# Pairs of half-height matmuls moved between rounds of an attention and feed-forward kernel, with another last projection unit and two more warm-up passes

## The chip, the core and the metric

The kernel runs on one core of a Trainium2 chip. Its time is the device time of one execution in microseconds; each number for a kernel is the median of several executions. Five engines work side by side and are tied by semaphores: TensorE (PE, with its weight loads listed apart as PEld), VectorE (DVE), ScalarE (ACT), GpSimd (POOL) and SyncE (SP). PE accumulates in PSUM, of which there are eight banks of 128 x 512 float32; SP and POOL issue most DMAs.

## The reference

The input x has 2048 rows of 448 numbers. The result mixes an attention block and a gated feed-forward block by a gate for each row:

```python
g = sigmoid((x * gate_w).sum(-1, keepdims=True))
# a: 16 heads of 28, softmax(q k^T * 28**-0.5) v, then @ wo
# b: gate = x @ W_gate; up = x @ W_up; (relu(gate) * up) @ W_down, F = 1792
return g * a + (1 - g) * b
```

## The kernel before

**Precision.** Operands of projections are split into a high part (rounded to the matmul's format, by a copy on ACT, or on DVE) and a low part (the difference, by DVE or POOL). A product of 448 rows is then a chain of eleven matmuls, the list TERMS, each of 128 rows and 512 columns. Chunk 6 of the weights holds the last 64 rows twice, high in one half of the partitions and low in the other. The last term, (6, 7), needs only 64 rows. Two such last terms ("tails") of two units can stand in different halves of the array: SECOND is the set of units whose tail lies in the second half and whose partner is the unit before. Such a pair starts nearly at once; other tails use all 128 rows.

**Projection.** After a memset on DVE, WARM matmuls on zeros run while the first data arrive and are split. Then come units qk(tb, c) (eleven matmuls of 512 columns into one bank, a copy on ACT, a low part on DVE, a send to DRAM by POOL) and vproj(tb, t) (eleven of 450 columns, a copy of V and one of the gate column, both on ACT; behind each fourth unit two sends of V by POOL). The list `mixed` sets their order: 19 qk and 16 vproj units, from the third on in turn. Between the matmuls of the later ones stand the first maxima of scores (smax: two matmuls into a double bank from ps_w, then a maximum over 1024 on DVE) and the first 16 scores (EARLY: one matmul into a bank from ps_s, then an exponential on ACT).

**Attention rounds.** ROUNDS lists strings, and each letter is one step in PE's order: s is a score matmul with its exponential, m a smax, x one pass of a gate/up unit (unit number 2i is gate of block i, 2i+1 is up), u the second half of the first weights' split, h the tails that were left out of the passes. A gate unit ends with a relu into RL, an up unit with spill_h: a product with RL on DVE, into a buffer h, and a send to DRAM by POOL. LONG and WIDE have maxima; LATE, the last three rounds, has none. There scores come in pairs (scores_pair: two matmuls into a double bank of ps_w, one exponential over 1024 columns), and relu runs on DVE. Behind the letters of a round split_f makes the weights for the next round, and pv multiplies the exponentials of eight tiles with V, in groups of four matmuls of 32 output columns each, and adds the sum po to os (DVE, or a copy by ACT for a head's first half).

**PSUM.** Three rings of two: ps_s and ps_x of one bank each, ps_w of two banks each. A new tile of a ring waits for the readers of the last but one.

**Behind the attention.** gate_up(i) computes gate and up of a block into one ps_w tile (blocks 51 to 55); down(i) multiplies a loaded and split hidden block (hh) with W_down into four accumulators acc (L703); wout multiplies the attention's result with wo, and result mixes.

Of the kernel before, what the change touches and what calls it, by code (L numbers as in the profile page):

```python
# [26 lines left out]
NF = F // P  # L27
NB = 4
# [2 lines left out]
SCALE = DH ** -0.5  # L31
VC = D + 2
NQ = 2 * D // P
WARM = 9

EARLY = (5, 5, 4, 4, 4, 3, 3, 3, 2, 2, 2, 2, 1, 1, 1, 1)

# [2 lines left out]

FIRST = "s" * 12 + "mmssmxxsxxusxmxsxsmxsmxsxsmxsxsmxsxsmxsxsxmsxsxmsxsxmsx"

LONG = "mxsmsxxxxxsmsxsmsxxsmsxsmsxxsmxxsmsxsxxsmsxxsxsmxsxsmsxxsmsxsmsxxsmsxsxxsmsmxssh"
WIDE = "sxxmxmxxsxxmsxxsxsmxxssxmxmxsxxsxxsxsmsxxsmxssxxxsmsxxsxmsxmsxsxmsxsmxsxsxxsmsxxsmsmsxxsxsh"

LATE = "ssxxxssxxxssxxxssxx" * 2 + "ssxxxssxxxssxxssxx" * 2 + "h"

ROUNDS = [(FIRST, 2)] + ([(LONG, 3)] * 2 + [(WIDE, 4)]) * 2 + [(LONG, 3)] * 2  # L50

ROUNDS += ([(WIDE, 4)] + [(LONG, 3)] * 8) * 2 + [(LONG, 3)] * 2 + [(LATE, 4)] * 3
NP = 9
# [4 lines left out]
NT = len(TERMS)  # L58
# [9 lines left out]
def gated_mix_kernel(ctx, tc, x, wq, wo, wgu, wd, out):  # L68
# [8 lines left out]
    def f32(ap):  # L77
        return ap.bitcast(F32)
# [4 lines left out]
    def ps_w(name):  # L83
        return psum.tile([P, 2, TB], F32, tag="mx", bufs=2, name=name)

    def ps_x(name):
        return psum.tile([P, TB], F32, tag="x", bufs=2, name=name)
# [7 lines left out]
    def low(dst, src, high):  # L95
        nc.vector.tensor_tensor(dst, src, f32(high), op=OP.subtract)  # L96
# [98 lines left out]
    def xf(tb, b):  # L195
        return X[tb][b // 4][:, b % 4]
# [13 lines left out]
    with tc.tile_pool(name="qkv", bufs=1) as pa:  # L210
# [127 lines left out]
        ps = ps_x("warm_ps")  # L338
        for n in range(WARM):
            nc.tensor.matmul(ps, warm[:, :P], warm, start=True, stop=True)  # L340
# [38 lines left out]
        units = [(qk, 3, 1), (qk, 2, 2), (qk, 3, 2)]  # L379
        units += [(qk, tb, c) for c in range(3, NQ) for tb in range(NB - 1, -1, -1)]  # L380
        vs = [(vproj, tb, t) for tb in range(NB - 1, -1, -1) for t in range(4)]
        mixed = units[:2]
        units = units[2:]
        while units or vs:
            mixed += units[:1] + vs[:1]
            units, vs = units[1:], vs[1:]
        spills = {15 + 3 * k: (NB - 1 - k // 2, k % 2) for k in range(6)}
        m, first, ahead = 0, 9, 2 * LEAD + 4
        for n, (f, *a) in enumerate(mixed):
# [15 lines left out]
            among, ends = [], m  # L405
# [21 lines left out]
    att = stk.enter_context(tc.tile_pool(name="att", bufs=1))  # L427

    done = sum(n for _, n in ROUNDS) // 2
    SECOND = {sum(n for _, n in ROUNDS[:r + 1]) - 1 for r in range(len(ROUNDS)) if "h" in ROUNDS[r][0]}  # L430
    SECOND |= set(range(2 * done + 1, 2 * NB * NF, 2))

    def lane(k):
        return slice(64 * k, 64 * k + 64)

    def split_f(i, high, low, part=(0, 1)):

        if part[0] == 0:
            WS[i] = fe.tile([P, 2, 7, P], F32R, name=f"wg_{i}", tag="wg", bufs=2)
        w, wr = WS[i], WR[i]  # L440
        for s in part:
            high(w[:, s, 0:3], wr[:, s, 0:3])
            low(w[:, s, 3:6], wr[:, s, 0:3], w[:, s, 0:3])
        if part[-1] == 1:
            high(w[:, :, 6], wr[:, :, 3])
            for s in range(2):
                rows = lane(1 - (2 * i + s in SECOND))
                low(w[rows, s, 6], wr[rows, s, 3], w[rows, s, 6])
            del WR[i]
# [4 lines left out]
    def gu_mm(ps, i, s, n):  # L454

        a, b = (BY_CHUNK if i else HIGH_FIRST)[n]
        rows = slice(0, P)
        if n == NT - 1 and 2 * i + s in SECOND | {k - 1 for k in SECOND}:
            rows = lane(int(2 * i + s in SECOND))
        nc.tensor.matmul(ps, WS[i][rows, s, a], xf(i // NF, b)[rows], start=(n == 0), stop=(n == NT - 1))  # L460
        c = b % 4
        if i % NF == NF - 1 and s and i < NB * NF - 1 and (n == NT - 1 or BY_CHUNK[n + 1][1] % 4 != c):
            for r in range(2):
                nc.sync.dma_start(f32(X[0][r])[:, c], x_d[i // NF + 1, r][:, c])
# [20 lines left out]
    NI = H * NK  # L485
    OS, LS = {}, {}

    def pv(i0, ni, late):

        h = i0 // NK  # L490
        po = ps_x(f"po_{i0}") if late else ps_w(f"po_{i0}")[:, 0]
        for i in range(i0, i0 + ni):
            p = PT.pop(i)
            for j in range(NB):
                nc.tensor.matmul(po[32 * j:32 * j + 32], V[:, h // 4 % 2, i % NK, h % 4], p[:, j], start=(i == i0),  # L495
                                 stop=(i == i0 + ni - 1))
        if i0 % NK == 0:
            OS[h] = fe.tile([P, TB], F32, name=f"os_{h}", tag="os", bufs=2)
            nc.scalar.activation(OS[h], po, AF.Copy)
        else:  # L500
            nc.vector.tensor_tensor(OS[h], po, OS[h], op=OP.add)  # L501
        if (i0 + ni) % NK == 0:
            LS[h] = fe.tile([P, 16], F32, name=f"ls_{h}", tag="ls", bufs=2)
            nc.gpsimd.dma_start(LS[h], OS[h][DH::32].rearrange("j (p c) -> j p c", c=16))
# [26 lines left out]
    def load_wo():  # L531
        r = f32(q_slot("wor"))
        nc.sync.dma_start(r[:, 0:3, :D], wo_d[0:3 * P].rearrange("(c p) n -> p c n", p=P))
        for a in (0, 64):
            nc.sync.dma_start(r[a:a + 64, 3, :D], wo_d[3 * P:])
        return r[:, :, :D]
# [7 lines left out]
    nxt = parts = i0 = 0  # L544

    def small_things(u):

        h, q = divmod(u, 4)

        if q == 0 and h and h + 2 < H:  # L550
            load_k(h + 2)
            load_q(h + 2)
        if u in (16, 32):
            g = u // 16 + 1
            nc.sync.dma_start(V[:, g % 2], v_d[g])
        if u == 1:
            gates()
        if u == 2:
            pack_wo()
        if h and q == 1:  # L560
            row_sums(h - 1)
            spread(h - 1)
        if h and q == 2:
            normalise(h - 1)
# [4 lines left out]
    for r, (order, nu) in enumerate(ROUNDS):  # L569
        ni = order.count("s") // NB  # L570
        late = order == LATE
        todo = list(range(nxt, nxt + nu))
        nxt += nu
        small_things(i0 // 4)
        if m % (2 * NK) == 0 and i0 <= NI - LEAD:
            smax_end(m // (2 * NK) - 1)
        if late and wor is None:
            wor = load_wo()

        passes = [(*divmod(k, 2), n) for k in todo for n in range(NT - ("h" in order and k >= nxt - 2))]  # L580
        units = []
        ns = 0
        for o in order:
            if o == "x" and not passes:
                continue
            if o == "s":
                i, j = i0 + 1 + ns // NB, ns % NB
                if ns == 4 * NB:
                    small_things(i0 // 4 + 1)
                if len(EARLY) <= i * NB + j < NI * NB and not late:  # L590
                    scores(i, j)
                elif late and i < NI and j % 2 == 0:
                    scores_pair(i, j)
                ns += 1
            elif o == "m":
                smax(m)
                m += 1
            elif o == "x":
                i, half, n = passes.pop(0)
                if n == 0:  # L600
                    ps = (ps_s if late else ps_x)(f"gu_{i}_{half}")
                    units.append((i, half, ps))
                gu_mm(units[-1][2], i, half, n)
                if n == NT - 1:
                    i, half, ps = units.pop()
                    spill_h(i, ps) if half else relu(i, ps, late)
            elif o == "u":
                split_f(0, act_high, pool_low, (1,))
                load_k(2)
                load_q(2)  # L610
                fetch_f(2)
                parts = 2
            elif o == "h":
                for i, half, ps in units:
                    gu_mm(ps, i, half, NT - 1)
                for i, half, ps in units:
                    spill_h(i, ps) if half else relu(i, ps, late)
        assert not passes, (r, passes)

        ready = nxt + (ROUNDS[r + 1][1] if r + 1 < len(ROUNDS) else 2)  # L620
        ready += ready % 2
        while parts < ready:
            split_f(parts // 2, dve_high if late else act_high, pool_low, (parts % 2,))
            parts += 1
            if parts % 2 == 0:
                fetch_f(parts // 2 + 1)
        pv(i0, ni, late)
        i0 += ni
        if late and i0 == NI:
            split_wo(wor)  # L630
# [35 lines left out]
    def gate_up(i):  # L666
        if i + 1 < NB * NF:
            split_f(i + 1, act_high, low)
        if i + 3 < NB * NF:
            fetch_f(i + 3)  # L670
        ps = ps_w(f"gu_{i}")
        for s in range(2):
            for n in range(NT - 1):
                gu_mm(ps[:, s], i, s, n)
        for s in range(2):
            gu_mm(ps[:, s], i, s, NT - 1)
        relu(i, ps[:, 0])
        spill_h(i, ps[:, 1])

# [51 lines left out]
    todo = [(gate_up, done), (row_sums, H - 1), (gate_up, done + 1)]  # L731
# [12 lines left out]
    for tb, load, split, at in ((0, 2, (3, 4), (5, 6, 7, 8)), (1, 5, (7, 9), (10, 11, 14, 14)), (2, 21, (23, 25), (28,) * 4),  # L744
                                (3, 35, (37, 39), (42,) * 4)):
        before(load, (fetch_o, tb))
        for k, i in enumerate(split):
            n = todo.index((down, i))
# [53 lines left out]
```

## Time and profile before

| | |
|---|---|
| median of 3 runs | 1299.31 us (1298.84 to 1300.36) |
| the profiled execution's own time | 1299.74 us |
| its span, first to last instruction | 1297.6 us |
| PE / DVE / ACT / POOL busy | 1290.2 / 817.3 / 763.0 / 367.3 us |
| matmuls | 6685 |
| lines of the chain with the largest shares | gu L460 22%, sm L152 19%, po L495 17%, s L178 17%, acc L703 11% |
| mean DMA rate | 115 GB/s |

Busy times are unions of the instructions of an engine in one profiled execution. Ends of matmuls are modelled, so their starts are the firmer reading. A row of the timeline gives the start, the length of a merged group, the engine, the line, the operation and its tiles; in brackets stands how long the engine was idle before it and what ended that. A row of the waits gives the total in us, how many times, and the longest.

In the trace the first pass on zeros starts at 1.20 us, the first projection matmul at 5.71, the attention's first round at 143.74, and its first pv at 161.22. The three LATE rounds run from 1018.3 to 1092.3; gate_up(51) starts at 1092.26.

### The profile page before, as it was taken

How to read it: one execution, taken by the hardware profiler on the slowest of the kernel's cores; microseconds unless marked ns; L12 is line 12 of the kernel's file. 1: busy time of each engine (PE TensorE's matmuls, PEld its weight loads, DVE VectorE, ACT ScalarE, POOL GpSimd, SP SyncE). 2: the span in 40 equal slices, each digit the busy share in tenths (PEclk: the TensorE clock that was granted, in tenths of full speed). 3: DMA queues.
4: the chain of work that ended last, by engine and by line, in shares of the span. 5: the costliest groups of instructions: out<-in, count | busy, mean ns of one | idle time of the engine just before them, and what ended most of it. 6: DMA issues, size and time to landing. Idle time of an engine off the chain costs nothing.

```text
span 1297.6 us, 17707 instructions
## 1 busy us (share of the span) xinstructions
PE 1290.2 (99%) x6685; PEld 901.8 (69%) x6685; DVE 817.3 (63%) x849; ACT 763.0 (59%) x1387; POOL 367.3 (28%) x551
## 2 busy tenths in 40 slices
PE   9999999999999999999999999999999999999998
PEld 6888766666666666666666666666666656899997
DVE  6487766667677676777666667767677333663342
ACT  5212776666767777777776666767676755322121
POOL 3222122332313222222223322313132354641020
PEclk9999999999999999999999999999999999999999
DMA  9845523151427223141535142422341222744432
GB/s 311 293 159 230 154 75 98 57 122 47 118 66 192 73 78 99 54 100 47 135 104 121 57 104 69 110 68 82 78 135 35 92 82 88 247 136 151 135 109 77
DMA packets 53565, 148.87 MB, mean 115 GB/s; under 512 B 10024, under 2 KB 17128, under 8 KB 48872
## 3 DMA queue, kind: packets, MB, share of 16 engines
q1 hardware_dynamic: 36120, 98.34, 28.3%
q0 software_dynamic: 16928, 48.93, 10.4%
q8 instruction: 53, 0.87, 0.3%
q10 hardware_dynamic: 432, 0.46, 0.1%
q14 instruction: 32, 0.26, 0.1%
HBM read 102.06 MB, written 46.02 MB: 114 GB/s over the span
## 4 chain that ended last, share of the span: by engine, by line
PE 99%; DMA 0%; ACT 0%; DVE 0%; issue 0%; ACTq 0%
PE gu L460 22%; PE sm L152 19%; PE po L495 17%; PE s L178 17%; PE acc L703 11%; PE qk L303 6%; PE v L313 3%; PE wo L657 3%; PE s L189 2%; DMA wr<-wq 0%; PE mt L162 0%; DVE mx L154 0%; DVE pair L96 0%; DVE y L709 0%; ACT pair L90 0%
## 5 line engine op out<-in xcount | busy, mean ns | idle before, releaser
L154 DVE TENSOR_REDUCE mx<-sm 128x1 f32<-128x1024 f32 x512 | 614.2, 1221 | 107.5 <-PE sm L152 107.3
L180 ACT ACTIVATE P<-s 128x512 f32<-128x512 f32 x724 | 414.8, 598 | 164.0 <-PE s L178 124.0
L460 PE MATMUL gu<-X,wg 128*128 128x512 f32 (+1 forms) x1232 | 392.3, 402 | 0.0
L178 PE MATMUL s<-Q,K 114*128 114x512 f32 x932 | 368.7, 401 | 0.0
L152 PE MATMUL sm<-K,Q 112*128 112x512 f32 x1024 | 324.0, 398 | 1.6 <-DVE mx L154 1.6
L460 PEld LDWEIGHTS gu<-X,wg 128*128 128x128 f32 (+1 forms) x1232 | 226.4, 189 | 55.3 <-issue 10.7
L178 PEld LDWEIGHTS s<-Q,K 114*128 114x128 f32 x932 | 175.2, 188 | 89.0 <-ACT P L180 47.7
L152 PEld LDWEIGHTS sm<-K,Q 112*128 112x128 f32 x1024 | 192.2, 190 | 46.9 <-issue 10.1
L495 PE MATMUL po<-P,V 128*32 128x512 f32 x1600 | 181.0, 594 | 0.0
L482 POOL DMA_DIRECT2D h_d<-h x56 | 31.6, 563 | 524.9 <-DVE h L476 441.0
L99 POOL TENSOR_TENSOR wg<-wgr,wg 128x384 fp32r<-128x384 f32 x204 | 146.8, 737 | 8.1
L180 ACT ACTIVATE V<-s 128x512 f32<-128x512 f32 x208 | 119.6, 598 | 42.0 <-PE s L178 30.4
L703 PE MATMUL acc<-WD,hh 128*128 128x448 f32 x672 | 141.1, 368 | 0.0
L703 PEld LDWEIGHTS acc<-WD,hh 128*128 128x128 f32 x672 | 125.8, 188 | 13.3 <-ACT wg L90 0.5
L495 PEld LDWEIGHTS po<-P,V 128*32 128x32 f32 x1600 | 49.5, 110 | 111.2 <-issue 110.5
L90 ACT ACTIVATE hh<-hr 128x512 fp32r<-128x512 f32 x56 | 35.4, 632 | 124.8 <-PE acc L703 119.4
L96 DVE TENSOR_TENSOR hh<-hr,hh 128x512 fp32r<-128x512 f32 x56 | 46.6, 832 | 65.7 <-ACT hh L90 65.7
L303 PE MATMUL qk<-X,W 128*128 128x512 f32 x308 | 79.7, 402 | 0.6 <-ACT X L90 0.5
L303 PEld LDWEIGHTS qk<-X,W 128*128 128x128 f32 x308 | 59.0, 193 | 15.6 <-ACT X L90 1.4
L501 DVE TENSOR_TENSOR os<-po,os 128x512 f32<-128x512 f32 x16 | 11.1, 691 | 86.2 <-PE po L495 81.3
L96 DVE TENSOR_TENSOR mh<-mr,mh 16x128 fp32r<-16x128 f32 x16 | 6.0, 375 | 90.8 <-ACT mh L166 90.8
L90 ACT ACTIVATE wg<-wgr 128x384 fp32r<-128x384 f32 x150 | 60.3, 491 | 2.4 <-DMA wgr<-wgu 2.4
(74 smaller groups left out, 767.1 us busy)
## 6 DMA issues: line engine op xcount, KB each, us to landing
wgr<-wgu SPq DMA_DIRECT2D x55, 512.0 KB
K<-qk_d SPq DMA_DIRECT2D x64, 224.0 KB
Q<-qk_d SPq DMA_DIRECT2D x64, 224.0 KB
h_d<-h POOLq DMA_DIRECT2D x56, 256.0 KB, 2.3
hr<-h_d SPq DMA_DIRECT2D x56, 256.0 KB
qk_d<-st POOLq DMA_DIRECT2D x21, 512.0 KB, 3.6
x_d<-X POOLq DMA_DIRECT2D x6, 1024.0 KB, 5.2
X<-x_d SPq DMA_DIRECT2D x24, 256.0 KB
```

Of the source, the lines that this page charges most:

```text
L90: nc.scalar.activation(dst, src, AF.Copy)
L96: nc.vector.tensor_tensor(dst, src, f32(high), op=OP.subtract)
L99: nc.gpsimd.tensor_tensor(dst, src, f32(high), op=OP.subtract)
L152: nc.tensor.matmul(ps[:, c, :], Q[h][:GD, u * P:(u + 1) * P], K[h % 3][:GD, k0:k0 + TB], start=True, stop=True)
L154: nc.vector.tensor_reduce(MX[h][:, 2 * u + half:2 * u + half + 1], ps, axis=AX.XY, op=OP.max)
L178: nc.tensor.matmul(ps, K[h % 3][:GD + 2, kt * P:(kt + 1) * P], Q[h][:GD + 2, j * TB:(j + 1) * TB], start=True, stop=True)
L180: nc.scalar.activation(PT[i][:, j], ps, AF.Exp, scale=SCALE)
L303: nc.tensor.matmul(ps, W[:, a, c * P:(c + 1) * P], xf(tb, b), start=(n == 0), stop=(n == NT - 1))
L313: nc.tensor.matmul(ps[:, :VC], xf(tb, b)[:, t * P:(t + 1) * P], W[:, a, 2 * D:], start=(n == 0), stop=(n == NT - 1))
L460: nc.tensor.matmul(ps, WS[i][rows, s, a], xf(i // NF, b)[rows], start=(n == 0), stop=(n == NT - 1))
L495: nc.tensor.matmul(po[32 * j:32 * j + 32], V[:, h // 4 % 2, i % NK, h % 4], p[:, j], start=(i == i0), stop=(i == i0 + ni - 1))
L703: nc.tensor.matmul(ACC[i // NF][t][:, :D], HH[i][:, a, t * P:(t + 1) * P], WD[:, f, b], start=(f == 0 and n == 0), stop=(f == NF - 1 and n ...
```

## The change

It does five things.

- WARM goes from 9 to 11.
- The last two units of `mixed` change places: qk(0, 6) comes before vproj(0, 3). FIRST has the same letters in another order.
- A LATE round leaves out the tails of all four units and does them at its end as two pairs, one for each h, so its string has 40 x instead of 42 and two h; the four strings in it become equal. Two of the four units accumulate in ps_s, two in ps_x (before, all in ps_s), and po of these rounds moves from ps_x to ps_w.
- SECOND holds no units behind the attention, and gate_up runs all eleven passes of gate and then of up.
- The high parts that are split for the next round in LATE are made by ACT instead of DVE.

```diff
-WARM = 9
+WARM = 11
...
-FIRST = "s" * 12 + "mmssmxxsxxusxmxsxsmxsmxsxsmxsxsmxsxsmxsxsxmsxsxmsxsxmsx"
+FIRST = "s" * 12 + "mmssxxxmsxxusxmsxmsxsxmsxsxmsxsxmsxsxmsxsxmsxsxmsxsxmsx"
...
-LATE = "ssxxxssxxxssxxxssxx" * 2 + "ssxxxssxxxssxxssxx" * 2 + "h"
+LATE = "ssxxxssxxxssxxssxx" * 4 + "hh"
...
         while units or vs:
             mixed += units[:1] + vs[:1]
             units, vs = units[1:], vs[1:]
+
+        mixed[-2:] = mixed[:-3:-1]
...
-    SECOND = {sum(n for _, n in ROUNDS[:r + 1]) - 1 for r in range(len(ROUNDS)) if "h" in ROUNDS[r][0]}
-    SECOND |= set(range(2 * done + 1, 2 * NB * NF, 2))
+    SECOND = {sum(n for _, n in ROUNDS[:r + 1]) - 1 - 2 * k for r in range(len(ROUNDS))
+              for k in range(ROUNDS[r][0].count("h"))}
...
-    def pv(i0, ni, late):
+    def pv(i0, ni):
...
-        po = ps_x(f"po_{i0}") if late else ps_w(f"po_{i0}")[:, 0]
+        po = ps_w(f"po_{i0}")[:, 0]
...
-        passes = [(*divmod(k, 2), n) for k in todo for n in range(NT - ("h" in order and k >= nxt - 2))]
+        passes = [(*divmod(k, 2), n) for k in todo for n in range(NT - (k >= nxt - 2 * order.count("h")))]
...
-                    ps = (ps_s if late else ps_x)(f"gu_{i}_{half}")
+                    ps = (ps_s if late and len(units) < 2 else ps_x)(f"gu_{i}_{half}")
...
             elif o == "h":
-                for i, half, ps in units:
+                ends, units = units[:2], units[2:]
+                for i, half, ps in ends:
                     gu_mm(ps, i, half, NT - 1)
-                for i, half, ps in units:
+                for i, half, ps in ends:
                     spill_h(i, ps) if half else relu(i, ps, late)
...
-            split_f(parts // 2, dve_high if late else act_high, pool_low, (parts % 2,))
+            split_f(parts // 2, act_high, pool_low, (parts % 2,))
...
-        pv(i0, ni, late)
+        pv(i0, ni)
...
         for s in range(2):
-            for n in range(NT - 1):
+            for n in range(NT):
                 gu_mm(ps[:, s], i, s, n)
-        for s in range(2):
-            gu_mm(ps[:, s], i, s, NT - 1)
         relu(i, ps[:, 0])
         spill_h(i, ps[:, 1])
```

## The prediction

> **What bounds the kernel.** I read the page first, then the waits of PE, then timelines of the places that the diff touches.
>
> ```profile
> span 1297.6 us, 17707 instructions
> PE 1290.2 (99%) x6685; PEld 901.8 (69%) x6685; DVE 817.3 (63%) x849; ACT 763.0 (59%) x1387; POOL 367.3 (28%) x551
> ...
> PE 99%; DMA 0%; ACT 0%; DVE 0%; issue 0%; ACTq 0%
> ```
>
> The chain is PE from end to end, so a change is worth what it does to the distances between matmul starts. By the timeline an ordinary 512-column matmul follows its predecessor by 233 ns, a 448-column one (L703) by 207. Whatever lets PE start later than that is listed here:
>
> ```profile
> PE sm L152 <- DVE mx L154: 1.6, 1, 1.6
> PE warm_ps L340 <- DVE warm L337: 1.2, 1, 1.2
> PE qk L303 <- ACT X L90: 0.5, 1, 0.5
> ```
>
> The large one is at the seam between projection and attention, here in the timeline (start, length, engine, work):
>
> ```profile
> 143.74 1.09 PE L152 MATMUL sm<-K,Q 112*128 112x512 f32 x4
> 144.44 0.60 ACT L90 ACTIVATE pair<-qk 128x512 fp32r<-128x512 f32 x1
> 144.91 0.53 ACT L90 ACTIVATE wg<-pair 128x384 fp32r<-128x384 f32 x1
> 145.07 0.69 DVE L96 TENSOR_TENSOR pair<-qk,pair 128x512 fp32r<-128x512 f32 x1 [1.79 <-ACT pair L90]
> 145.68 3.47 DVE L154 TENSOR_REDUCE mx<-sm 128x1 f32<-128x1024 f32 x3
> 146.94 0.73 PE L152 MATMUL sm<-K,Q 112*128 112x512 f32 x2 [1.64 <-DVE mx L154]
> ```
>
> The last projection unit, qk(0,6), ends; ACT copies it only after the exponentials queued ahead; DVE's low half waits for that copy 1.79 us, and the maxima stand behind it on DVE. PE needs the third maximum's bank, free only at 146.9.
>
> The second kind of loss has no waits; it shows in the weight loads (PEld):
>
> ```profile
> 1060.78 0.19 PEld L460 LDWEIGHTS gu<-X,wg 64*128 64x128 f32 x2 [0.37 <-issue]
> 1061.22 0.16 PEld L495 LDWEIGHTS po<-V 128*32 128x32 f32 x8 [0.25 <-issue]
> ...
> 1097.14 0.19 PEld L460 LDWEIGHTS gu<-X,wg 64*128 64x128 f32 x2 [0.37 <-issue]
> 1097.57 1.47 PEld L460 LDWEIGHTS gu<-X,wg 128*128 128x128 f32 x7 [0.25 <-issue]
> ```
>
> Where the shape of the array changes, the load isn't done ahead. Behind the attention the starts are: full 1096.81, pair of half-height tails 1097.14 (3 ns apart), full 1097.57, full 1097.91: 328+3+430+338 = 1099 ns.
>
> **Part by part.** The profiled execution took 1299.74 us, its span 1297.60 and 2.14 around it; it lies 0.43 above the median of the runs, 1299.31.
>
> *A unit of v last, and the new FIRST.* Of the 2037 ns between the starts at 144.91 and 146.945, 1.80 us is loss, and the next distance (335) adds 0.10. With vproj last, nothing of it goes to DVE. The low half of qk(0,6) is now issued a unit earlier, where DVE idled for 1.10 us (139.31 to 140.41): I place it at about 140.8 to 141.5, the two maxima of the last unit behind it to 143.8, and those of the first "mm" at 144.2 to 146.5. The third comes after "ssxxx", at 146.2 instead of 145.1; it needs the first bank, free at 145.4. New on ACT: v's copy (0.54) and the gate column (0.18) for qk's copy (0.60), so the first weights' high half stays at about 145.47, while PE now wants it at 145.14: loss about 0.38. On POOL, two v_d sends (0.57 and 0.56 at 140.80 and 141.36) replace one of 0.72 ahead of the weights' low half, which ends near 147.1; the first pass with it, the seventh, comes at 148.6. The counts of FIRST are equal (32 s, 12 m, 22 x). Sum 1.90 - 0.38 = **1.5 us**; bounds 0.9 (two more stalls like the 0.3) and 1.9 (none).
>
> *Two pairs in LATE.* Per round two full tails (2 x 233 = 466 ns) leave the stream, and a second pair stands behind the first. The distance X between pairs isn't in this trace. Lower row: 226 to 233, the stream without a change of shape, where PEld starts the next load 2 ns after a matmul starts (as po's groups do in their own shape). Upper row: 430, pair to other shape. I take 230: the shape stays. Per round 466 - 233 = 0.23 us, three times 0.70. Against it: "xx" follows "xx" twice in every string now, and the pair behind such a place started 27 ns late (1056.45 to 1056.72); three or four more of these are 0.1. **0.6 us**; bounds 0.0 and 0.7.
>
> *No pairs behind the attention.* Unit 51: 1099 ns become 4 x 233 = 932, a gain of 0.167. Units 52 to 55, each in front of L703: 328+3+422+307 = 1060 become 3 x 233 + 207 = 906, 0.154 each. Sum 0.78. But the first down step is close to its data:
>
> ```profile
> 1101.65 0.63 ACT L90 ACTIVATE hh<-hr 128x512 fp32r<-128x512 f32 x1 [3.37 <-DMA hr<-h_d]
> 1102.31 0.91 DVE L96 TENSOR_TENSOR hh<-hr,hh 128x512 fp32r<-128x512 f32 x1 [0.93 <-ACT hh L90]
> 1102.88 1.49 PE L703 MATMUL acc<-WD,hh 128*128 128x448 f32 x6
> ```
>
> Its third matmul (1103.39) uses what DVE finishes at 1103.22, a chain that goes back over hr's load to the split of wo behind the last pv. PE would be there 0.32 earlier, of which 0.15 to 0.2 is waited for. **0.6 us**; bounds 0.5 and 0.78. The other four have more than 1 us.
>
> *Eleven passes.* The clock shows in the number of matmuls:
>
> ```profile
> 6.30:9.70 3.40, 3.40 (x9) 2.60 (x8) 3.32 (x8) 2.80 (x8) 0.65 (x3) 1.00 1.01 336
> 9.70:13.10 3.40, 3.40 (x16) 2.57 (x15) 2.97 (x6) 3.08 (x7) 0.89 (x1) 1.00 0.77 266
> 9.44 1.42 DVE L96 TENSOR_TENSOR W<-wr,W 128x336 fp32r<-128x336 f32 x4
> ```
>
> Until 9.7 us starts are 427 ns apart, then 233 (the granted share reads 1.00 in both). The ninth pass starts at 4.58, the first real matmul at 5.71 after 0.49 idle; two more passes fill that and put it at 5.86. If PE then runs fast from about 6.3, it gains little: the second unit's weights come from DVE (the row at 9.44; its second instruction ends at 10.37), and its second matmul already starts at 10.43. What is left is the 0.10 in the next distance of 333 ns. If in other executions PE gets fast later, each microsecond costs 1 - 233/427 = 0.45, and a stretch of 3.4 us 1.5, as much as the runs differ (1.52). I take **0.25**, near this profile; bounds 0 and 1.2.
>
> The Trainium skill ("TensorE: Matmul & The Clock Gate", Part 1) says that a free-running window of 3.41 us has to be busy before the clock doubles. By that rule the gap at 5.2 to 5.7 cost this execution a window, and the phase varies by run: the eleven would be worth 0.1 here and up to 1.5 elsewhere. The change from 427 to 233 at 9.7 agrees; the phase no single trace shows.
>
> *At nothing.* The copies of LATE's weights go from DVE to ACT: six (0.51, 0.51 and 0.40 per unit) in ACT's idle 7.5 us under pv (1036.47 to 1044.02); without that cover the next exponential would be late by up to 2.4 us. POOL has two sends of h, each behind a product on DVE, ahead of the low halves; these start some 4.1 us behind the first tail instead of 2.9, the first is done at 5.1, and the next round's second pass wants it at 8.9. po moves into the ring of score pairs: the second pair of the next round needs it 1.69 us after the last po group starts, and the sum leaves it at 1.35 (1042.72 to 1044.07).
>
> Sum 1.5 + 0.6 + 0.6 + 0.25 = 2.95: the profiled execution at 1296.8, the median at 1299.31 - 2.95 = **1296.4 us**.
>
> **Rivals.**
> 1. *The second pair can't load ahead.* X is 430, LATE gives 0.03 and not 0.6: 1296.9. For it: after each pair PEld idles 0.25. Against it: that is where the shape changes. Beside this stands a rule of the same page of the Trainium skill, Part 3: weight loads overlap running matmuls only when the row groups differ, and the third tail uses the rows of the first. The loads 2 ns behind each full-height start speak against it. Chance 0.12.
> 2. *The seam's wait only changes its name.* The exponentials of the last four scores and v's copy keep ACT longer, first weights come at 146.5, or the low half reaches DVE so late that maxima still hold PE: the seam gives 0.5, 1297.4. Chance 0.11.
> 3. *The clock falls back.* Between 6.3 and 10.4 a fast PE waits often for data; should the grant fall for 3.41 us from 9.7, that costs 1.4: 1297.8. For it: nothing but the late rise behind a gap of 0.49. Chance 0.07.
> 4. *Slower: po holds the score pairs.* If sum and products queue so that po's bank stays full, PE stands in front of the second pair of the second and third LATE round. Slack is 0.34; the kernel is slower from 1.5 + 0.34 late at each, and by 0.2% from (2.95 + 2.6)/2 + 0.34 = 3.1: 1302. Against it: two maxima with zero and two products take 3 us of the 7.4 under pv. Chance 0.07.
> 5. The change not doing what it says, leaving the pairs' number or places as they were, is excluded by the code of SECOND and of the passes.
>
> **How the numbers follow.** About 0.2%, 2.6 us, can be told from no change. The forecast has 0.63; its gain of 2.95 is close to that bound, but unknown ends (the seam 1.9, the clock 1.2) reach further up than down, so 0.57 of it is faster and 0.06 within. Rival 1 gives 0.03 faster, 0.09 within; 2 and 3 are within, 4 slower. Faster 0.60, same 0.33, slower 0.07. All upper bounds together give 4.6 us (1294.7), all lower 1.4 (1297.9); for 8 in 10 I take 1294.9 to 1298.2, which holds rivals 1 to 3.
>
> **What would show it.** Right: no wait of PE on maxima near 145 but one of some 0.4 on ACT's weights; four half-height loads in each LATE round, the second two some 230 ns behind the first; no half-height load behind the attention; the step from 427 to 233 ns near 6.3. Wrong: those loads 430 apart; a wait of score pairs on the sum of po; a new wait of PE after 145 of over a microsecond.

## The result, and the profile after

The changed kernel takes 1302.36 us (median of 11 executions, 1300.58 to 1303.86), the kernel before 1299.33 beside it. The ratio is 1.0022 with a 95% interval of [1.0013, 1.0031]: 3.0 us slower, where 2.95 us faster was forecast, and outside the range. The profiled execution took 1303.86 us, its span 1302.1; it is the longest of the eleven, 1.5 us above their median.

The page and the waits of PE, in the same order as before:

```profile
span 1302.1 us, 17712 instructions
PE 1290.5 (99%) x6687; PEld 902.4 (69%) x6687; DVE 807.5 (62%) x834; ACT 768.0 (59%) x1402; POOL 365.3 (28%) x551
...
PE 96%; DMA 1%; POOL 1%; issue 0%; ACT 0%; SPq 0%; DVE 0%; ACTq 0%; POOLq 0%
PE gu L462 21%; PE sm L152 18%; PE s L178 17%; PE po L497 17%; PE acc L704 11%; PE qk L303 5%; PE wo L660 3%; PE v L313 3%; PE s L189 2%; DMA v_d<-V 1%; DMA wr<-wq 0%; POOL WO L99 0%; PE mt L162 0%; DMA hr<-h_d 0%; POOL wg L99 0%
```

```profile
PE s L178 <- ACT V L180: 5.4, 1, 5.4
PE warm_ps L340 <- DVE warm L337: 1.2, 1, 1.2
PE gu L462 <- ACT wg L90: 0.2, 1, 0.2
PE qk L303 <- DVE X L96: 0.2, 1, 0.2
```

A DMA, `v_d<-V`, now has 1% of the chain, and PE has one wait of 5.4 us that it didn't have. The wait on maxima (1.6) is gone, as forecast. The timeline shows where the new wait comes from:

```profile
145.38 1.11 POOL L321 DMA_DIRECT2D v_d<-V  x2 [2.73 <-ACT zt L318]
...
154.86 1.09 ACT L180 ACTIVATE V<-s 128x512 f32<-128x512 f32 x2 [5.63 <-DMA v_d<-V]
155.51 0.80 PE L178 MATMUL s<-Q,K 114*128 114x512 f32 x1 [5.42 <-ACT V L180]
```

The exponentials that PE waits for are written into V. p_slot gives tiles 5 and 6 of every nine the place of V's groups 2 and 3, free once these groups have been sent to DRAM. With vproj(0, 3) last, the sends are issued at 145.4 instead of 140.8, ACT is ready to write at 149.2, and the data are not read out before 154.8. The stretch behind the wait shows a second price (columns: us, PE, PEld, DVE, ACT and POOL busy with their counts, granted clock, DMA share, GB/s):

```profile
149.00:155.50 6.50, 1.10 (x5) 0.57 (x3) 2.59 (x5) 0.87 (x4) 1.31 (x3) 0.91 0.93 217
155.50:161.00 5.50, 5.49 (x13) 4.33 (x14) 2.04 (x2) 3.12 (x6) 0.00 (x0) 0.50 0.85 164
```

From 154.31 to 161.14 PE was granted half its clock: 13 matmuls in 5.5 us instead of some 24.

The profiled executions side by side, from the starts of matmuls; a stretch ends where the first matmul behind it starts (a minus is a gain):

| stretch | before | changed | difference | forecast |
|---|---|---|---|---|
| to the end of the projection | 143.50 | 143.53 | +0.03 | -0.25 |
| from there to the first pv | 17.72 | 24.46 | +6.74 | -1.5 |
| to the pv ahead of LATE (28 rounds) | 850.05 | 848.34 | -1.71 | 0 |
| LATE, to gate_up(51) | 80.99 | 80.43 | -0.56 | -0.6 |
| gate_up(51) to the last gate/up matmul | 33.83 | 33.79 | -0.04 | -0.6 |
| rest of the span | 171.55 | 171.54 | 0.0 | 0 |

### The profile page after: what moved, and what is told of

Read it like the earlier page. It is cut to its first block, busy times and chain, and to the rows that moved or that the text cites. A ratio compares the mean times of both kernels' runs of the same rounds, so it can differ in the third digit from the quotient of the medians.

```text
span 1302.1 us, 17712 instructions
## 1 busy us (share of the span) xinstructions
PE 1290.5 (99%) x6687; PEld 902.4 (69%) x6687; DVE 807.5 (62%) x834; ACT 768.0 (59%) x1402; POOL 365.3 (28%) x551
## 4 chain that ended last, share of the span: by engine, by line
PE 96%; DMA 1%; POOL 1%; issue 0%; ACT 0%; SPq 0%; DVE 0%; ACTq 0%; POOLq 0%
PE gu L462 21%; PE sm L152 18%; PE s L178 17%; PE po L497 17%; PE acc L704 11%; PE qk L303 5%; PE wo L660 3%; PE v L313 3%; PE s L189 2%; DMA v_d<-V 1%; DMA wr<-wq 0%; POOL WO L99 0%; PE mt L162 0%; DMA hr<-h_d 0%; POOL wg L99 0%
## 5 line engine op out<-in xcount | busy, mean ns | idle before, releaser
L90 ACT ACTIVATE wg<-wgr 128x384 fp32r<-128x384 f32 x165 | 66.3, 491 | 4.1 <-DMA wgr<-wgu 2.9
```

The lines of the kernel that those rows point to most:

```text
L90: nc.scalar.activation(dst, src, AF.Copy)
```

## The experiments

**The edit alone, and all but it.** The first kernel undoes the two edits of the seam, as shown; the second is the kernel before with these two only, so with the lines the other way round:

```diff
-FIRST = "s" * 12 + "mmssxxxmsxxusxmsxmsxsxmsxsxmsxsxmsxsxmsxsxmsxsxmsxsxmsx"
+FIRST = "s" * 12 + "mmssmxxsxxusxmxsxsmxsmxsxsmxsxsmxsxsmxsxsxmsxsxmsxsxmsx"
...
-        mixed[-2:] = mixed[:-3:-1]
```

> The changed kernel with the old order of the last two projection units and the old FIRST. Theory (the seam alone costs: exponentials into V's groups 2 and 3 wait for the late v_d sends, and the clock falls behind that): the seam is as in the kernel before, with its wait of 1.6 us on maxima, and the LATE rounds keep their gain of 0.56 us; 0.6 below the kernel before, 0.0 to 1.0. If the 1.7 us that the rounds with maxima gained belong to the other edits, 2.3 below. Rival (the eleven passes or the pairs cost too): 1 us or more above the kernel before.

Measured: 1298.63 against 1298.69, ratio 0.9995 [0.9986, 1.0004]. LATE is again 0.60 shorter (80.39). The wait of 1.6 us on maxima is back, and in this profile half a clock follows it, which the profile of the kernel before didn't have:

```profile
148.47:151.88 3.41, 3.41 (x10) 2.64 (x9) 1.75 (x2) 2.02 (x6) 1.88 (x3) 0.50 0.83 180
```

The gain of 0.6 us that was expected is less than the interval can tell from none.

> The kernel before with only the two units changed in place and the new FIRST. Theory: the whole loss is here, a wait of 5 to 6 us of PE near 150 us, behind it 3.4 or 6.8 us at half the clock; span at the first pv 6 to 7 us later than before; 3 to 7 us above the kernel before (the smaller, if the gain of the rounds with maxima comes with it). Rival: within 1 us of the kernel before.

Measured: 1302.92 against 1298.69, ratio 1.0032 [1.0020, 1.0043]. Its seam takes 21.25 us, with this row among the waits of PE:

```profile
PE s L178 <- ACT V L180: 3.2, 1, 3.2
```

So the loss lies in the seam alone. In this execution the wait is shorter than the 5 to 6 us that I expected and half the clock lasts 3.4 us, so the first pv is 3.0 us late, not 6 to 7; the median is 4.2 us up.

**Another place for the exponentials.**

```diff
-        if k in (5, 6):
-            return V[:, k - 3].rearrange("p k h d -> p (k h d)").rearrange("p (j t) -> p j t", t=TB)
+        if k in (7, 8):
+            return V[:, k - 5].rearrange("p k h d -> p (k h d)").rearrange("p (j t) -> p j t", t=TB)
```

> The changed kernel, but the exponentials of tiles 5 and 6 of nine go to buffers of their own and those of tiles 7 and 8 to V's groups 2 and 3, which are so first written two tiles (some 5 us) later. Theory (the wait is for the send of V to be read out): no wait of PE over 1 us near 150, no half clock behind it, the first pv near 159.7 instead of 168.0; 8 us below the changed kernel, near 1294.5. If the sends land at 154.9 as they did and the first such exponential is due at 155.5, nothing is left of the wait; if the sends are later, up to 1 us. Rival (ACT is late for another reason, such as the longer queue on ACT): the wait stays, 1302.

Measured: 1295.96, ratio 0.9979 [0.9970, 0.9987]. No wait of PE over 0.2 us is left near 150, and the same two stretches read:

```profile
149.00:155.50 6.50, 6.50 (x30) 5.15 (x29) 6.26 (x9) 5.46 (x13) 1.27 (x3) 1.00 0.93 250
155.50:161.00 5.50, 5.50 (x31) 3.65 (x33) 4.92 (x6) 4.58 (x10) 0.00 (x0) 1.00 0.42 115
```

The seam takes 16.30 us, 1.42 less than before: nearly what the prediction had for it. The gain over the changed kernel is 8.2 us in the seam of the profiles, as expected, but some 5.6 us by the two ratios: the 28 rounds took 850.05 here, 1.71 more, and the changed kernel's profile is 1.5 us above its median. The send of group 2 lands at 152.31, 7.0 us behind its issue, and the first exponential into it starts at 154.57, 2.3 us later. This margin isn't always there: in another profile with these places (the one with the pairs, further down) the two are 154.20 and 154.44.

**PE kept busy while it waits.** 24 matmuls on zeros ahead of the score that waits:

```diff
+    fill = ps_x("fill_ps")
...
+                if r == 0 and len(passes) == 14:
+                    for _ in range(24):
+                        nc.tensor.matmul(fill, warm[:, :P], warm, start=True, stop=True)
```

> The changed kernel with 24 matmuls on zeros (some 5.2 us at 216 ns) into a bank of their own, put on PE just ahead of the score that waits. The wait on ACT stays, so PE goes on at the same moment, but has not stood still. Theory (standing still cost the clock): no distances of 427 ns behind 155 us, granted clock 1.0 in that stretch, 2.5 us below the changed kernel (1299.8). Rival (the clock fell for another reason, or costs nothing): 1302.4, with half the clock as before.

Measured: 1300.64, ratio 1.0014 [1.0005, 1.0023]. The same windows, and the filling in the timeline (one of its 24 records is missing):

```profile
149.00:155.50 6.50, 6.43 (x31) 3.32 (x31) 2.01 (x5) 1.60 (x3) 0.81 (x2) 1.00 0.95 232
155.50:161.00 5.50, 5.50 (x25) 4.51 (x24) 4.79 (x4) 4.64 (x10) 0.00 (x0) 1.00 0.51 119
```

```profile
149.58 5.13 PE L609 MATMUL fill_ps<-warm 128*128 128x512 bf16 x23
```

ACT still waited 3.85 us for the sends, but the clock stayed at 1.00. The filling was longer than this wait, so the seam's 21.45 us hold 5.2 us of it and no half clock; of the 3.0 us less than in the changed kernel's seam a part belongs to the shorter wait. Standing still is what costs the clock; how much of the median that is, this run doesn't separate. By the ratios it is 1.0 us below the changed kernel, where 2.5 were expected, and the two intervals overlap.

**Why the sends take so long.** Two runs. In the first, less data is sent last:

```diff
-            if t == 3:
+            if t == 3 or (tb == 0 and t == 2):
+                k0 = k if tb == 0 and t == 3 else k - t
...
-                    nc.gpsimd.dma_start(v_d[g][:, k - 3:k + 1], V[:, g, k - 3:k + 1])
+                    nc.gpsimd.dma_start(v_d[g][:, k0:k + 1], V[:, g, k0:k + 1])
```

> The changed kernel (exponentials of tiles 5 and 6 into V's groups 2 and 3 again), with the last send of each group of v split in two: the first three tiles of 64 KB each go behind vproj(0,2), some 9 us earlier, and only the last tile behind vproj(0,3). Theory A (the send lands 9 us behind its issue because it shares the DMA engines with the loads of K, Q and weights, so less data lands sooner): landing within 5 us, the wait of PE falls from 5.4 to 1 or less and the clock stays, 1295.5 to 1297. Theory B (the time is latency or the order in a queue, whatever the size): the wait stays at 4 to 5.4 us, 1301 to 1302.

Measured: ratio 1.0023 [1.0014, 1.0032], wait of PE 3.3 us, which is neither theory's figure. But whole sends left a wait of 3.2 us too (the kernel with the two edits only), and a quarter of the data still lands 7.3 us behind its issue: less data alone doesn't bring it forward. In the second, SP's loads of K are taken out of the way:

```diff
-    def load_k(h):
+    def load_k(h, queue=nc.sync):
...
-            nc.sync.dma_start(f32(K[h % 3])[DH * r:DH * (r + 1)], qk_d[r % 2, 2 * DH * h:2 * DH * h + DH, :])
+            queue.dma_start(f32(K[h % 3])[DH * r:DH * (r + 1)], qk_d[r % 2, 2 * DH * h:2 * DH * h + DH, :])
...
-                load_k(2)
+                load_k(2, nc.gpsimd)
```

> The changed kernel, exponentials of tiles 5 and 6 into V's groups 2 and 3 as there, v sent whole; only the four loads of K for head 2 (224 KB each) are issued by POOL, behind the sends of v in its queue, instead of by SP at 144.1 us. Theory (in the trace of the changed kernel the sends' packets trickle at one tenth of their rate while SP's loads of K, Q and weights fill the DMA engines, 9.6 us to landing instead of 2.9): the sends land by 149, at the latest 150.5, no wait of PE for exponentials over 0.5 us, no half clock, 8 us less at the first pv, 0.998 of the kernel before. Rival (size and sharing don't matter, as the split send suggests): landing stays at 7 us or more, 1.002 of the kernel before.

Measured: 1295.93, ratio 0.9974 [0.9965, 0.9983], no wait of PE over 0.2 us. The view of the DMAs near the seam (issues: size, us to landing; queues: packets, MB, share of the engines), first the kernel before, then the changed one, then this one:

```profile
v_d<-V POOLq DMA_DIRECT2D x2, 256.0 KB, 2.9
```

```profile
q1 hardware_dynamic: 408, 1.99, 77.2%
q0 software_dynamic: 225, 0.73, 19.0%
v_d<-V POOLq DMA_DIRECT2D x2, 256.0 KB, 9.6
```

```profile
q0 software_dynamic: 394, 1.47, 36.0%
K<-qk_d POOLq DMA_DIRECT2D x4, 224.0 KB, 8.5
v_d<-V POOLq DMA_DIRECT2D x2, 256.0 KB, 3.1
```

Before, POOL's sends (q0) went out in 141 to 144 us, while SP's queue (q1) had nothing. In the changed kernel they meet SP's loads of K, 4 x 224 KB from 144.1 on, and one load of weights. With K's loads behind them in their own queue they need 3.1 us again, though the load of weights is still in SP's. The Trainium skill ("DMA: Bandwidth & Descriptors", Queues, rings and completion order) says that an engine takes turns between queues and serves a whole packet of some 9 to 17 descriptors before it changes. In the changed kernel's trace the pieces of 8 KB in SP's queue took 0.5 to 0.9 us each from 146 to 151.5 us (the middle half of them), so by that rule a single turn is, as an estimate, 9 x 0.5 = 4.5 us or more, and a smaller send gains little. The split send agrees with its 7.3 us; the packets' bounds are in no trace here.

**Eleven passes, and the pairs behind the attention**, both on the kernel with the exchanged slots:

```diff
-WARM = 11
+WARM = 9
```

> The kernel with the exchanged slots (1295.96), with nine passes instead of eleven. Theory now (the start is set by the data's splits on DVE, and the passes only fill): the first v unit starts at the same time within the spread of the five profiles so far (37.87 to 38.47), 1296.0, within 0.4. Theory of the prediction: 0.25 slower, up to 1.2 in executions in which the clock rises late, 1296.2 to 1296.6.

Measured: ratio 0.9977 [0.9968, 0.9986], beside 0.9979 with eleven (on another chip, so only ratios compare). The projection ended at 142.95, and in the other profiles at 142.95 to 143.83, with nine passes or eleven.

```diff
+    SECOND |= set(range(2 * done + 1, 2 * NB * NF, 2))
...
-            for n in range(NT):
+            for n in range(NT - 1):
...
+        for s in range(2):
+            gu_mm(ps[:, s], i, s, NT - 1)
```

> The kernel with the exchanged slots, with the five pairs of tails behind the attention back as before. By the sum of the prediction 0.6 us slower (0.78 less 0.2 of wait); by the trace of the changed kernel, where the wait of the first down step took nearly all of it, the stretch from gate_up(51) to the end is the same within 0.1 us, and the median within 0.3.

Measured: ratio 0.9977 [0.9968, 0.9986]. The stretch from gate_up(51) on takes 34.05 us with the pairs and 33.91 without: 0.14, not 0.6, and even that is within what profiles differ by. Three profiles with the pairs have 33.83 to 34.05, nine without them 33.70 to 34.00.

**The first down step.** The split of wo goes ahead of the last pv:

```diff
+        if late and i0 + ni == NI:
+            split_wo(wor)
         pv(i0, ni)
         i0 += ni
-        if late and i0 == NI:
-            split_wo(wor)
```

> The kernel with the exchanged slots, with the split of wo issued ahead of the last pv instead of behind it, so that POOL makes its low half beside pv and the loads of the first hidden block don't wait for it. Theory (the first down step waits for hh, whose load waits for buffers that the split of wo reads): the loads start some 2.5 us earlier, the distance of 548 ns and the two of 305 and 312 at the first down step become 207, the stretch behind the attention 0.5 us shorter, 1295.4. Rival (the loads wait for pv's own buffers, or hh is late for another reason): no change; if the later send of the row sums is missed further on, up to 1 us slower.

Measured: ratio 0.9973 [0.9962, 0.9984]; the stretch takes 33.30 us, 0.61 less than with the exchanged slots alone and below all twelve of the profiles just named; this shows in the profile, not in the ratio. In the changed kernel the first down step waits twice:

```profile
1106.51 0.63 ACT L90 ACTIVATE hh<-hr 128x512 fp32r<-128x512 f32 x1 [3.69 <-DMA hr<-h_d]
1107.17 0.82 DVE L96 TENSOR_TENSOR hh<-hr,hh 128x512 fp32r<-128x512 f32 x1 [1.02 <-ACT hh L90]
1107.19 0.50 PEld L704 LDWEIGHTS acc<-WD,hh 128*128 128x128 f32 x2 [0.29 <-ACT hh L90]
...
1108.05 1.10 PEld L704 LDWEIGHTS acc<-WD,hh 128*128 128x128 f32 x6 [0.36 <-DVE hh L96]
```

With the split of wo early, POOL starts its low half 0.4 us ahead of gate_up(51) (1089.71 and 1090.12) and not 2.0 behind it (1098.74 and 1096.76 in the changed kernel), the loads of hr go out 2.2 us earlier with it, and the down step runs through:

```profile
1098.42 0.69 DVE L96 TENSOR_TENSOR hh<-hr,hh 128x512 fp32r<-128x512 f32 x1 [0.63 <-ACT hh L90]
...
1100.29 2.49 PEld L704 LDWEIGHTS acc<-WD,hh 128*128 128x128 f32 x12
```

**Together, and two profiles again.**

> The loads of K for head 2 on POOL's queue and the split of wo ahead of the last pv, together. Theory: the two gains lie in different stages and add, 0.9974 less 0.5 us (0.0004): 0.997 of the kernel before, between 0.996 and 0.9975. Rival (the early split of wo gains only where something else was late): 0.9974.

Measured: 1296.48 against 1300.45, ratio 0.9968 [0.9956, 0.9980], the lowest ratio of all, though its interval holds 0.9974 too. In its profile both gains are there: the seam takes 16.24 us, and the stretch from gate_up(51) on 33.30.

> The changed kernel, unaltered, profiled once more. In its first profile the 28 rounds from the first to the last pv ahead of LATE took 848.3 us, against 850.1 in the kernel before and in seven of the nine others. If that belongs to the execution, 850.1 or 848.3 may come now; if it belongs to the kernel, 848.3 again.

> The kernel with the loads of K for head 2 on POOL's queue, profiled once more; its first profile had 848.7 us for the same 28 rounds. If that belongs to the execution, 850.1 may come now; if to the kernel, 848.7 again.

Measured: the changed kernel again 848.35 us for the 28 rounds, but the kernel with K's loads on POOL 850.06, where its first profile had 848.72. So one kernel can show either time. Against the kernel before, the changed kernel's first profile is shorter by 0.04 to 0.11 us in every LONG round and longer by 0.02 to 0.04 in the WIDE ones, so nothing single happens there. Which of the two an execution takes, and why, stays open; the edits don't decide it alone. The second profile of the changed kernel has a wait of PE of 4.6 us and again 6.8 us of half clock.

## Why the prediction was wrong, step by step

*A unit of v last.* Wrong, and this is the whole loss. The step that failed is the one on POOL: "two v_d sends (0.57 and 0.56 at 140.80 and 141.36) replace one of 0.72 ahead of the weights' low half". It counted what the sends cost in POOL's queue and not who waits for their landing. The code and the profile before both had the answer: p_slot puts tiles 5 and 6 into V, and rows with `V<-s` were on the page. Even then the price had to be found: at the 2.9 us to landing of the kernel before, the sends would have ended near 148.8, ahead of the 149.2 at which ACT wanted the place. The rest is contention with SP's loads, into whose time the sends had been moved. The seam's 24.46 us are 16.30 (the run with other slots), 5.42 of wait, and 5.63 us at 427 instead of 233 ns per matmul, 2.55; 0.2 is left. None of the rivals had this: rival 2 looked for a new wait in the same place, but on the weights; rival 3 let the clock fall, but in the first 13 us. Among the signs of being wrong stood "a new wait of PE after 145 of over a microsecond"; it came, but with no price in the forecast.

The rest of that step held. The low half of qk(0,6) ran from 140.94 (forecast 140.8), PE's wait on the first weights cost 612 - 233 = 0.38 us (0.38), and without the new wait the seam gained 1.42 (1.5).

*Two pairs in LATE.* Right in the sum. The weights of the second pair are loaded 0.1 us behind the first pair; the matmuls follow 335 ns behind it, not 230, and po 323 behind them, not 430. The two differences cancel, so the sum is right by luck:

```profile
1040.38 0.30 PEld L462 LDWEIGHTS gu<-X,wg 64*128 64x128 f32 x4 [0.37 <-issue]
1041.04 0.16 PEld L497 LDWEIGHTS po<-P,V 128*32 128x32 f32 x8 [0.37 <-ACT V L191]
```

LATE gained 0.56 or 0.60 in seven profiles (forecast 0.6), but 0.31 in five others, four with the exchanged slots and the one with the split send: there the second of the three rounds was 0.10 us longer than before, and why stays open. The rule of rival 1, no loading ahead on the same rows, doesn't hold here: these loads start while the first pair, on those rows, still runs.

*No pairs behind the attention.* The mechanism was right and the term mis-sized: the tails gain, but the wait of the first down step, put at 0.15 to 0.2, took 0.54 (312, 548 and 305 ns in place of 207), of which some 0.05 comes back behind it. Most of the difference is the first load of hr: from its issue to its first use it took 2.71 us in the profile of before (1098.94 to 1101.65) and 3.02 in the changed kernel (1103.49 to 1106.51). With the loads released earlier the stretch is 0.53 shorter than before, and 0.04 with the wait. The tails themselves were also put a little high: behind each pair the next matmuls of L703 in the profile of before came 203 ns apart on the mean, not 207, and so won back a part of its cost.

*Eleven passes.* Nothing to be seen: start and median agree within the spread. In all profiles the granted clock's record starts where the distances drop from 427 ns: at 4.1 to 7.0 us in the eleven profiles with eleven passes, at 5.1, 6.4 and 9.7 in the three with nine. The first v unit starts at 37.85 to 38.74 in all of them (38.30 in the profile of before), so the late rise there cost nothing that lasted. Nor is it shown that the gap of 0.49 us kept the clock down: in the changed kernel's profile it rose at 4.12, and the 3.41 us ahead of that begin 0.48 before the first pass.

That the runs differ by 1.52 us, which the prediction put down to this rise, rather belongs to the seam. In the fifteen executions of the kernel before beside the run with K's loads on POOL, the eight with a mean granted clock of 1.0 took 1298.4 to 1299.0, the seven with less 1300.0 to 1301.0; the eleven of that run, which has no wait of 1.6 us, lie within 0.8. This fits 3.41 us at half clock behind the wait, seen once in a profile (the first experiment); for the executions that weren't profiled it is not shown.

*At nothing.* Held: no wait on po's bank, on the copies moved to ACT, or on POOL's low halves.

## What to carry to other kernels

When a step is moved, list the buffers that its DMAs still read, and look for who writes these next: the send's landing, not its issue, ends the lifetime. A landing time belongs to the stretch in which it was measured: moved under another queue's loads, the same transfer took three times as long here. And a wait of PE has a price beyond its length where the clock falls behind it, so a new wait of 5 us can cost 8.

## What the hardware showed that I had not expected

- The clock fell for 3.41 us in whole steps: none behind the 1.6 us wait in the profile of before, 3.41 behind a wait of the same length in the first experiment and behind 3.2 and 3.3 us, 6.83 behind 4.6 and 5.4. The same wait can so cost 1.5 us more or nothing. In all five traces with a fall near 150 us it comes a whole number of steps of 3.413 us behind the clock's first rise (42 to 44 of them). Counted so, the wait of 1.6 us lay within one step in the first experiment (145.3 to 147.0, the step 145.06 to 148.47) and across the end of one in the profile of before (146.24); that this decides is a reading of two traces.
- 256 KB that took 2.9 us to land took 9.6 beside another queue's loads (7.0 to 9.9 over the profiles), and a quarter of it still 7.3.
- 28 rounds of equal instructions took 850.0 us in ten profiles and 848.3 to 848.7 in four, without a wait that tells them apart; it stays open.
